# Attention feeding two MLPs on one core: the last double pair's sums first, six w_in blocks before the second batch, and a longer lead of w_in's products over w_out's

## The chip, the cores and the metric

The kernel runs on one core of a Trainium2 chip. The metric is the device time of one execution in microseconds, lower is better. TensorE multiplies into eight PSUM banks, VectorE, ScalarE and GpSimd do the elementwise work, and SyncE starts all DMA transfers. In the rows below they are PE (PEld is its weight load), DVE, ACT, POOL and SP.

## The reference

Two batches of 448 tokens, 12 heads of 64 columns; then two MLPs over all 896 tokens.

```python
scores = cap * tanh((q @ k.T) / sqrt(64) / cap)
attn   = exp(scores); attn = attn / (attn.sum(-1) + 1e-9)     # up to a common factor
x      = (attn @ v) heads side by side                         # 896 x 768
h      = x @ w_in                                              # 768 -> 2048
g      = (a0 + a1*h + a2*h**2 + a3*h**3) / (1 + |b0|*|h| + |b1|*h**2 + 1e-6)
x2     = g @ w_out                                             # 2048 -> 768
y      = max(x2 @ w1, x2 @ w2, x2 @ w3) @ w_out2               # 768 -> 768 -> 768
```

## The kernel before

**Number formats.** The MLP weights arrive as 64-bit floats. `weight()` loads a block of 128 x 768 into one of three `raw` buffers and decodes it on the chip: `scale` (L400 ScalarE or L402 GpSimd), `shift` (L406 VectorE), `rest` (L422 ScalarE or L425 VectorE), `sign` (L415 VectorE), a rounded high copy `wh...` (L441) and the remainder `wl...` (L430). Activations are split the same way, x into a high copy (L642) and a remainder (L646), g into `gh` (L745) and `gl` (L748). Each product of the MLPs is three matmuls: high by high, high by low, low by high.

**Attention** goes in six *double pairs* d of four heads each, d = 0 to 2 for batch 0 and 3 to 5 for batch 1. For each: six score tiles and one tile of the ends (L515, L522), tanh and exp on ScalarE (L536, L539, the tiles e_0 to e_6), the weighted values (L556, L575) into two banks that are copied to `xu` (L586), and the sums of the exponentials by a matmul with ones (L599, `summed`). The sums take a round trip: copied to a `row` buffer (L609), written to DRAM (`sums`), read back spread over the partitions (`comp`), inverted on VectorE (L617, L618), written to DRAM again (`rsum`), and read with a broadcast into two `row` buffers by four DMAs (`row<-rsum`). Then `scale` multiplies xu by the row (L638) and splits it into the two blocks of x of that double pair (L642, L646): d = 5 makes x_4 and x_5 of batch 1. All these DMAs, and the loads of `raw`, start in one order on SyncE.

**First MLP.** w_in is cut into 16 blocks fc of 128 columns; a *unit* is one block for one batch, 18 matmuls at L666 (`up`), two at a time over blocks of x. A unit's bank is read by ScalarE (L683, L686) and VectorE (L697, L700); L700, `second`, is the last reader, and only then another unit can use the bank. Two units together go through `rational` (L721 to L731) and `parts` (gh, gl). `down` multiplies them with w_out (L773): half "oa" runs between the units, half "ob" after all of them. The constant NG is the number of w_in blocks that batch 0 runs before batch 1 starts on the same blocks; LAG says how many pairs of units `up` runs ahead of `down`.

**The second MLP** (L861, L921) follows and isn't touched.

**Order.** The kernel doesn't write its engines' orders by hand. Each operation is added to `Flow` with an estimated cost on each engine that could do it; `Flow` derives due times, picks engine and buffer, and issues on each engine in the order it plans. TensorE's order follows the order of adding. `place` says which banks a value may use: once all scores are done, "h" (units) and "acc" may use any bank, "av" (weighted values and sums) only banks 4 and 5.

Of the kernel before, what the change touches and what calls it, by code (L numbers as in the profile page):

```python
# [17 lines left out]
B, H, S, D = 2, 12, 448, 64  # L18
# [9 lines left out]
GUARD = 1e-9  # L28
QGUARD = 1.0 + 1e-6
CAP = 6  # L30
NG = 4
LAG = 3
NSLOT, NRAW, NROW = 51, 3, 4
ND = NPAIR // 2
NFULL = S // P
# [35 lines left out]
class Flow:  # L71
# [11 lines left out]
    def add(self, engines, fn, after=(), vals=(), shared=False, due=None, leave=0, ahead=1e9, size=0.0, mode=None):  # L83
        first = next(iter(engines))
        if first == "pe":
            due = self.clock
            self.clock += engines["pe"]
        after = [a for a in after if a is not None]
        op = Op(engines, after, list(dict.fromkeys(vals)), fn, shared, due, leave, ahead, size, mode)
        for v in op.vals:  # L90
            v.users += 1
        for a in op.after:
            a.next.append(op)
        op.left = len(op.after)
        self.ops.append(op)
        return op

    def place(self, v, but=()):
        if v.kind not in ("sc", "av", "h", "acc"):
            free = self.free[v.kind]  # L100
            return (free[0],) if free else None
        done = self.scores == 0
        if v.kind == "sc":
            order = [(2 * i, 2 * i + 1) for i in ((0, 1, 3) if v.early else (0, 1))]
        elif done:
            order = [(4,), (5,)] if v.kind == "av" else [(i,) for i in range(8)]
        else:
            order = {"av": [(4,), (5,)], "h": [(6,), (7,)], "acc": []}[v.kind]
        order = [at for at in order if not any(self.banks[i] or i in but for i in at)]
        return min(order, key=lambda at: max(self.freed[i] for i in at)) if order else None  # L110
# [180 lines left out]
def attention_moe(ctx: ExitStack, tc: tile.TileContext, qk, v, w_in, w_out, w123, w_out2, par, out):  # L291
# [44 lines left out]
    def bank(val):  # L336
        return singles[val.at[0]]
# [4 lines left out]
    def dma(out_, in_, after=(), vals=(), size=0.0, issue=0.4, **kw):  # L342
        return add({"sp": issue}, lambda e: nc.sync.dma_start(out=out_(), in_=in_()), after, vals, size=size, **kw)  # L343
# [108 lines left out]

    units = [(fc, b) for b in range(B) for fc in range(NG)]
    units += [(fc, b) for fc in range(NG, NFC) for b in range(B)]
    NU = len(units)
    NK = NU // 2
    for n in range(NG):
        weight(("in", n), w_in[n])
        if n % 2:
            weight(("oa", n // 2), w_out[0, n // 2])  # L460
    for j in range(NG // 2, NFC // 2):
        weight(("in", 2 * j), w_in[2 * j])
# [14 lines left out]
    comp = [cp.tile([P, NG2], F32, name=f"comp{g}") for g in range(B * ND)]  # L477
# [70 lines left out]
    def weighted_rest(d):  # L548
        vr, got_v = VV[d]
        o = [Val("av", f"av{d}_{r}") for r in range(2)]  # L550
        x, ex = E[d, 2 * NFULL]

        def products(e):
            for r in range(2):
                for j in range(2):
                    pe.matmul(  # L556
                        bank(o[r])[j * D : j * D + D, :S], rest(vr, r, j), two(x)[r * D : r * D + D, j],
                        start=True, stop=False,
                    )

        done = add({"pe": FULL}, products, [ex, got_v], [*o, x, vr], mode="both")
        AV[d] = o, done
        XU[d] = slot(f"xu{d}"), []
        for c in last_copy[-2:]:
            c.before(done)

    def weighted(d, r):
        vr, got_v = VV[d]
        o, dep = AV[d][0][r], AV[d][1]
        es = [E[d, r * NFULL + n] for n in range(NFULL)]  # L570

        def products(e):
            for n, (x, _) in enumerate(es):
                for j in range(2):
                    pe.matmul(  # L575
                        bank(o)[j * D : j * D + D, :S], whole(vr, n, r, j), two(x)[:, j], start=False,
                        stop=n == NFULL - 1,
                    )

        dep = add(  # L580
            {"pe": NFULL * FULL}, products, [got_v, dep] + [ex for _, ex in es], [o, vr] + [x for x, _ in es],
            mode="halves",
        )
        xu, parts = XU[d]
        parts.append(add(
            {"dve": 0.54, "act": 0.43}, lambda e: copy_on[e](two(xu)[:, r], bank(o)[:, :S]), [dep], [o, xu]  # L586
        ))

    def summed(d):
        t, row = Val("av", f"sm{d}"), Val("row", f"sr{d}")  # L590
        es = [E[d, i] for i in range(2 * NFULL + 1)]

        def products(e):
            for n in range(NFULL + 1):
                for r in range(2):
                    x = es[r * NFULL + n if n < NFULL else 2 * NFULL][0]
                    for j in range(2):
                        g = (2 * r + j) * Q
                        pe.matmul(  # L599
                            bank(t)[g : g + Q, :S], ones[:, 0 if n < NFULL else 1 + r], two(x)[:, j], start=n == 0,  # L600
                            stop=n == NFULL, tile_position=(0, g),
                        )

        dep = add(
            {"pe": (NFULL + 1) * FULL}, products, [ex for _, ex in es] + [filled], [t] + [x for x, _ in es],
            mode="quarters",
        )
        got = add(
            {"act": 0.43, "dve": 0.54}, lambda e: copy_on[e](rows[row.at[0]], bank(t)[:, :S]), [dep], [t, row]  # L609
        )  # L610
        last_copy.append(got)
        flat_ = sums[d].rearrange("g s -> (g s)").rearrange("(p k) -> p k", p=P)
        out_ = dma(lambda: sums[d], lambda: rows[row.at[0]][0:P:Q], [got], [row], size=0.007, issue=0.4)
        back = dma(lambda: comp[d], lambda: flat_, [out_], size=0.007, issue=0.4)

        def recip(e):
            dve.tensor_scalar(out=comp[d], in0=comp[d], scalar1=guard, scalar2=None, op0=ALU.add)  # L617
            dve.reciprocal(out=comp[d], in_=comp[d])  # L618

        rc = add({"dve": 0.4}, recip, [back, guard_in])  # L620
        dst = rsum[d].rearrange("r j s -> (r j s)").rearrange("(p k) -> p k", p=P)
        wrote = dma(lambda: dst, lambda: comp[d], [rc], size=0.007, issue=0.4)
        for r in range(2):
            scale(d, r, wrote)

    def scale(d, r, wrote):
        xu, parts = XU[d]
        b, p = divmod(2 * d + r, NPAIR)
        row, x = Val("row", f"row{d}_{r}"), slot(f"x{b}_{p}", F32R)
        got = []  # L630
        for j in range(2):
            rr = slice(j * D, j * D + D)
            src = rsum[d][r, j : j + 1].broadcast_to([D, S])
            got.append(dma(lambda rr=rr: rows[row.at[0]][rr], lambda src=src: src, [wrote], [row], size=0.115, issue=0.4))
        u = lambda: two(xu)[:, r]
        m = add(
            {"dve": 0.54, "pool": 1.1},
            lambda e: engine[e].tensor_tensor(out=u(), in0=u(), in1=rows[row.at[0]], op=ALU.mult),  # L638
            [*got, *parts], [xu, row], shared=True,
        )  # L640
        hi = add(
            {"act": 0.47, "dve": 0.30}, lambda e: copy_on[e](two(x)[:, 0], u()), [m], [x, xu], shared=True,  # L642
        )

        def low(e):
            engine[e].tensor_tensor(out=two(x)[:, 1], in0=u(), in1=f32(two(x)[:, 0]), op=ALU.subtract)  # L646

        X[b, p] = x, add({"dve": 0.54, "pool": 1.1}, low, [hi], [x, xu], shared=True)
# [152 lines left out]
    for d in range(B * ND):  # L801
        for r in range(2):
            prep(2 * d + r)
        values(d)
        scores(d, 2 * NFULL)
        if d:
            weighted_rest(d - 1)
        for n in range(NFULL):
            scores(d, 2 * n)
            scores(d, 2 * n + 1)  # L810
            if d:
                weighted(d - 1, n) if n < 2 else summed(d - 1)
    table = add({"act": 1.3}, lambda e: act.preload_act_table_set("natural_log_exp_and_others"), last_tanh)
    early = 0
    weighted_rest(B * ND - 1)
    for j in range(2):
        up(early)
        early += 1
        weighted(B * ND - 1, j)
    summed(B * ND - 1)  # L820
    for n in range(early, 2 * LAG):
        up(n)
    for k in range(NK):
        parts(k)
        if k + LAG < NK:
            up(2 * (k + LAG))
            up(2 * (k + LAG) + 1)
        down("oa", 2 * k, 0)
# [163 lines left out]
```

## Time and profile before

| | |
|---|---|
| Time, median of three runs | 521.52 us (520.74 to 524.95) |
| The profiled execution's own time | 524.37 us |
| Its span, first to last instruction | 522.6 us |
| TensorE busy | 510.7 us (98%), 2637 matmuls |
| VectorE busy | 358.8 us (69%) |
| ScalarE busy | 295.1 us (56%) |
| GpSimd busy | 47.4 us (9%) |
| Mean granted clock of TensorE | 0.997 |

A time is that of the whole execution; the span leaves out 1.77 us before the first and after the last instruction. Shares are over the whole span: VectorE's 69% is an average of stretches where it is nearly always busy and of a last third where it is nearly idle.

### The profile page before, as it was taken

To read this page: it belongs to the slowest core of one execution; us is meant where nothing else is said; L and a number is where in the kernel's file an instruction comes from. 1 tells how busy PE (TensorE), PEld (TensorE's weight loads), DVE (VectorE), ACT (ScalarE), POOL (GpSimd) and SP (SyncE) were. 2 spreads that over 40 slices of the span, in tenths; PEclk is the share of its full clock that TensorE was granted. 3 is DMA by queue.
4 is the path that set the end of the run, shared out by engine and by line. 5 is a ranking of instruction groups with operands and counts; after the bars stand their busy time and mean duration, and the time that the engine had idled before them with its cause. 6 is when DMAs were issued, how large, how long until landed. Compare 5 with 4: busy or idle time off the path is not lost.

```text
span 522.6 us, 6706 instructions
## 1 busy us (share of the span) xinstructions
PE 510.7 (98%) x2637; PEld 418.0 (80%) x2637; DVE 358.8 (69%) x494; ACT 295.1 (56%) x407; POOL 47.4 (9%) x48
## 2 busy tenths in 40 slices
PE   8899999997999999999999999999999999999997
PEld 5333333676899889999997999999999999999996
DVE  0267999989999998788899999999842417111000
ACT  6999999956778866466766553474621121101111
POOL 0202303001201120101010200100000000000000
PEclk9999999999899999999999999999999999999999
DMA  8956755344101112000013678768400000000211
GB/s 308 365 181 217 243 180 212 111 156 154 62 0 61 60 61 60 1 1 2 1 61 99 217 251 279 249 210 271 176 0 2 0 1 0 1 0 10 80 64 61
DMA packets 16448, 58.37 MB, mean 112 GB/s; under 512 B 3592, under 2 KB 6944, under 8 KB 16416
## 3 DMA queue, kind: packets, MB, share of 16 engines
q1 hardware_dynamic: 16416, 57.94, 32.4%
q8 instruction: 20, 0.33, 0.3%
q14 instruction: 12, 0.10, 0.1%
HBM read 55.10 MB, written 2.84 MB: 111 GB/s over the span
## 4 chain that ended last, share of the span: by engine, by line
PE 60%; DVE 18%; DMA 9%; ACT 8%; issue 2%; SPq 2%; DVEq 0%; ACTq 0%
PE b L861 25%; PE b L773 16%; PE b L666 11%; PE b L921 8%; ACT e L536 4%; DMA rsum<-comp 3%; ACT e L539 3%; DMA row<-rsum 3%; SPq L343 2%; DVE W L697 2%; DMA comp<-sums 2%; DVE W L700 2%; DVE W L728 2%; DVE T L725 2%; DVE W L731 1%
## 5 line engine op out<-in xcount | busy, mean ns | idle before, releaser
L861 PE MATMUL b<-x,whm 128*128 128x448 f32 x432 | 122.6, 365 | 0.0
L666 PE MATMUL b<-x,whin 128*128 128x448 f32 x384 | 112.4, 373 | 2.7 <-DVE x L646 1.4
L861 PEld LDWEIGHTS b<-x,whm 128*128 128x128 f32 x432 | 81.1, 188 | 6.4
L666 PEld LDWEIGHTS b<-x,whin 128*128 128x128 f32 x384 | 72.4, 190 | 14.2 <-issue 3.0
L861 PE MATMUL b<-x,wlm 128*128 128x448 f32 x216 | 78.9, 365 | 0.0
L666 PE MATMUL b<-x,wlin 128*128 128x448 f32 x192 | 71.2, 371 | 0.0
L536 ACT ACTIVATE e<-b,qscale 128x448 f32<-128x448 f32 x84 | 49.0, 811 | 2.3 <-PE b L515 2.3
L889 ACT CAST h3h<-t 128x448 fp32r<-128x448 f32 x12 | 6.8, 567 | 66.8 <-DVE t L884 66.7
L539 ACT ACTIVATE e<-e,con 128x896 f32<-128x896 f32 x42 | 44.3, 1249 | 0.0
L861 PEld LDWEIGHTS b<-x,wlm 128*128 128x128 f32 x216 | 40.6, 188 | 3.2
L666 PEld LDWEIGHTS b<-x,wlin 128*128 128x128 f32 x192 | 36.5, 190 | 3.6
L773 PE MATMUL b<-gl,whoa 128*128 128x448 f32 x96 | 35.5, 369 | 2.2 <-DVE gl L748 2.2
L773 PE MATMUL b<-gh,wloa 128*128 128x448 f32 x96 | 35.2, 367 | 0.0
L773 PE MATMUL b<-gh,whoa 128*128 128x448 f32 x96 | 35.2, 367 | 0.0
L773 PE MATMUL b<-gh,whob 128*128 128x448 f32 x96 | 35.2, 366 | 0.0
L515 PE MATMUL b<-qk 64*128 64x448 f32 x144 | 33.6, 564 | 1.6 <-ACT e L536 1.4
L773 PE MATMUL b<-gh,wlob 128*128 128x448 f32 x96 | 35.1, 365 | 0.0
L773 PE MATMUL b<-gl,whob 128*128 128x448 f32 x96 | 35.1, 365 | 0.0
L686 ACT ACTIVATE W<-b,con 128x448 f32<-128x448 f32 x32 | 23.0, 719 | 18.6 <-PE b L666 18.5
L879 DVE TENSOR_TENSOR t<-b,t 128x448 f32<-128x448 f32 x12 | 7.5, 622 | 33.9 <-PE b L861 33.8
L515 PEld LDWEIGHTS b<-qk 64*128 64x128 f32 x144 | 14.3, 186 | 20.1 <-ACT e L536 9.5
L575 PE MATMUL b<-e,v 128*64 128x448 f32 x144 | 29.0, 545 | 0.0
(111 smaller groups left out, 917.7 us busy)
## 6 DMA issues: line engine op xcount, KB each, us to landing
raw<-in_w_out_dram SPq DMA_DIRECT2D x22, 768.0 KB, 4.4
raw<-in_w_dram SPq DMA_DIRECT2D x18, 768.0 KB, 4.2
raw<-in_w_in_dram SPq DMA_DIRECT2D x16, 768.0 KB, 6.0
qk<-in_qk_dram SPq DMA_DIRECT2D x12, 448.0 KB, 7.7
v<-in_v_dram SPq DMA_DIRECT2D x6, 448.0 KB, 11.9
row<-rsum SPq DMA_DIRECT2D x24, 112.0 KB, 3.6
out_dram<-ob SPq DMA_DIRECT2D x6, 384.0 KB, 2.8
out_dram<-ob SPq DMA_DIRECT2D x2, 192.0 KB, 1.9
```

The lines of the kernel that those rows point to most:

```text
L343: return add({"sp": issue}, lambda e: nc.sync.dma_start(out=out_(), in_=in_()), after, vals, size=size, **kw)
L515: pe.matmul(pair(t, j)[:, :S], k[rr], q[rr], start=True, stop=True)
L536: act.activation(two(x)[:, j], pair(t, j)[:, :S], AF.Tanh, scale=qscale)
L539: act.activation(two(x), two(x), AF.Exp, scale=cap)
L575: pe.matmul(bank(o)[j * D : j * D + D, :S], whole(vr, n, r, j), two(x)[:, j], start=False, stop=n == NFULL - 1,)
L666: pe.matmul(bank(h)[:, :S], w_, x_, start=cc == 0 and i == 0, stop=cc == NCC - 1 and i == len(terms) - 1)
L686: act.activation(two(w_)[:, i], bank(h)[:, :S], AF.Identity, bias=a2, scale=a3)
L697: dve.tensor_tensor(out=two(w_)[:, i], in0=bank(h)[:, :S], in1=two(w_)[:, i], op=ALU.mult)
L700: dve.scalar_tensor_tensor(out=two(w_)[:, i], in0=two(w_)[:, i], scalar=a1, in1=bank(h)[:, :S], op0=ALU.add, op1=ALU.mult)
L773: pe.matmul(bank(a)[:, :S], w_, g_, start=count[half, o, b] == 1, stop=count[half, o, b] == 3 * NFC)
L861: pe.matmul(bank(o)[:, :S], w_, x_, start=cc == 0 and i == 0, stop=cc == NCC - 1 and i == 2)
L921: pe.matmul(bank(o)[:, :NH], h_, w_, start=i == 0, stop=i == len(terms) - 1)
```

## The change

Four edits. NG goes from 4 to 6 and LAG from 3 to 4. After the scores, "av" values may use any bank. For the last double pair, one unit instead of two is run before the sums; the sums (`summed`) are added before the two weighted products instead of after them, and the scaling is split from `summed`, so that it is added after the weighted products. Elsewhere `summed` and `scale` stand one behind the other as before. The functions' lines from L619 on stand two lines lower in the changed kernel (L638 becomes L640, L666 becomes L668, L773 becomes L775).

```diff
-NG = 4
-LAG = 3
+NG = 6
+LAG = 4
@@ place
         elif done:
-            order = [(4,), (5,)] if v.kind == "av" else [(i,) for i in range(8)]
+            order = [(i,) for i in range(8)]
@@ summed(d)
-        wrote = dma(lambda: dst, lambda: comp[d], [rc], size=0.007, issue=0.4)
-        for r in range(2):
-            scale(d, r, wrote)
-
-    def scale(d, r, wrote):
+        return dma(lambda: dst, lambda: comp[d], [rc], size=0.007, issue=0.4)
+
+    def scale(d, wrote):
+        for r in range(2):
+            scale_pair(d, r, wrote)
+
+    def scale_pair(d, r, wrote):
@@ the double pairs
             if d:
-                weighted(d - 1, n) if n < 2 else summed(d - 1)
+                if n < 2:
+                    weighted(d - 1, n)
+                else:
+                    scale(d - 1, summed(d - 1))
 ...
     weighted_rest(B * ND - 1)
+    up(early)
+    early += 1
+    wrote = summed(B * ND - 1)
     for j in range(2):
-        up(early)
-        early += 1
         weighted(B * ND - 1, j)
-    summed(B * ND - 1)
+    scale(B * ND - 1, wrote)
     for n in range(early, 2 * LAG):
```

On TensorE, at the last double pair, the order before is this: weighted values into banks 85 and 86, six matmuls that end unit 1 (b_88, left out here) and six that begin unit 2, then the sums in bank 85.

```order
L575 MATMUL b_86<-e_3_754,v_499 64x448 x2
L575 MATMUL b_86<-e_4_770,v_499 64x448 x2
L575 MATMUL b_86<-e_5_795,v_499 64x448 x2
...
L666 MATMUL b_81<-x_1_480,whin_571 128x448 x2
L666 MATMUL b_81<-x_1_480,wlin_579 128x448
L599 MATMUL b_85<-e_0_682,ones 32x448 x2
L599 MATMUL b_85<-e_3_754,ones 32x448 x2
```

In the changed kernel at the same place:

```order
L668 MATMUL b_87<-x_5_662,wlin_416 128x448
L599 MATMUL b_81<-e_0_682,ones 32x448 x2
L599 MATMUL b_81<-e_3_740,ones 32x448 x2
...
L599 MATMUL b_81<-e_6_670,ones 32x448 x4
L575 MATMUL b_85<-e_0_682,v_495 64x448 x2
...
L575 MATMUL b_86<-e_5_785,v_495 64x448 x2
```

The sums stand right behind the last matmuls of unit 0, in bank 81, and the weighted values behind them.

On SyncE, from the write of the sums of d = 5 (sums_94) to the broadcast reads of its inverses (rsum_100), the order before is this; comp_106 is d = 5's, raw_... are loads of weights.

```order
L343 DMA sums_94<-row_80 4x448
L343 DMA raw_75<-in_w_in_dram 128x1536
L343 DMA comp_106<-sums_94 128x14
L343 DMA raw_74<-in_w_out_dram 128x1536
L343 DMA raw_76<-in_w_in_dram 128x1536
L343 DMA rsum_100<-comp_106 128x14
L343 DMA row_77<-rsum_100 64x448 x2
L343 DMA row_78<-rsum_100 64x448 x2
```

In the changed kernel from the read-back of d = 4 (comp_105) on:

```order
L343 DMA comp_105<-sums_93 128x14
L343 DMA raw_75<-in_w_in_dram 128x1536
L343 DMA sums_94<-row_78 4x448
L343 DMA rsum_99<-comp_105 128x14
L343 DMA raw_76<-in_w_out_dram 128x1536
L343 DMA comp_106<-sums_94 128x14
L343 DMA row_79<-rsum_99 64x448 x2
L343 DMA row_80<-rsum_99 64x448 x2
L343 DMA raw_74<-in_w_in_dram 128x1536
L343 DMA rsum_100<-comp_106 128x14
L343 DMA raw_75<-in_w_in_dram 128x1536
L343 DMA row_77<-rsum_100 64x448 x2
```

The round trips of d = 4 and d = 5 are now interleaved, with four loads of weights between the steps; a load waits for VectorE to have read that buffer's last block.

On VectorE, around the remainder of x_5 of batch 1 (the last step of d = 5), the order before is this.

```order
L638 TENSOR_TENSOR xu_863<-xu_863,row_77 128x448
L638 TENSOR_TENSOR xu_863<-xu_863,row_78 128x448
L725 SCALAR_TENSOR_TENSOR T_972<-T_972,qone,A_970 128x896
L646 TENSOR_TENSOR x_4_1065<-xu_863,x_4_1065 128x448
L646 TENSOR_TENSOR x_5_1068<-xu_863,x_5_1068 128x448
```

And in the changed kernel:

```order
L640 TENSOR_TENSOR xu_874<-xu_874,row_77 128x448
L727 SCALAR_TENSOR_TENSOR T_846<-T_846,qone,A_842 128x896
L699 TENSOR_TENSOR W_959<-b_83,W_959 128x448
L640 TENSOR_TENSOR xu_874<-xu_874,row_78 128x448
L702 SCALAR_TENSOR_TENSOR W_959<-W_959,con,b_83 128x448
L694 TENSOR_SCALAR T_980<-A_964,absb 128x448
L644 CAST x_5_1032<-xu_874 128x448
L730 SCALAR_TENSOR_TENSOR W_840<-W_840,con,A_842 128x896
L699 TENSOR_TENSOR W_1030<-b_84,W_1030 128x448
L648 TENSOR_TENSOR x_5_1032<-xu_874,x_5_1032 128x448
```

Six instructions of the MLP now stand between the second multiplication (L638, now L640) and the remainder of x_5, where one stood; and the multiplication itself has moved up: from the copy of the sums of d = 3 (the row `L609 ... row_78<-b_85`) to the remainder of x_5, VectorE's list has 71 instructions instead of 79.

## Rows read from the trace of the kernel before

**Rows 1.** What TensorE waits for, whole span: total us, times, longest.

```profile
PE b L773 <- DVE gl L748: 2.2, 2, 1.1
...
PE b L666 <- DVE W L700: 0.5, 2, 0.3
```

**Rows 2.** TensorE, 122 to 135 us: start, duration, line, and the idle time before.

```profile
122.29 0.37 PE L773 MATMUL b<-gh,whoa 128*128 128x448 f32 x1
123.75 0.47 PE L773 MATMUL b<-gl,whoa 128*128 128x448 f32 x1 [1.10 <-DVE gl L748]
...
125.52 0.37 PE L773 MATMUL b<-gh,whoa 128*128 128x448 f32 x1
...
127.79 0.37 PE L773 MATMUL b<-gh,wloa 128*128 128x448 f32 x1
128.97 0.47 PE L666 MATMUL b<-x,whin 128*128 128x448 f32 x1 [0.81 <-ACT x L642]
130.84 0.70 PE L666 MATMUL b<-x,whin 128*128 128x448 f32 x1 [1.40 <-DVE x L646]
...
131.71 0.95 PE L666 MATMUL b<-x,whin 128*128 128x448 f32 x2
...
134.54 0.37 PE L666 MATMUL b<-x,wlin 128*128 128x448 f32 x1
```

**Rows 3.** TensorE, the ends' weighted values of two double pairs.

```profile
74.67 1.69 PE L556 MATMUL b<-e,v 64*64 64x448 f32 x8
...
88.46 0.98 PE L556 MATMUL b<-e,v 64*64 64x448 f32 x8
```

**Rows 4.** Busy time of the engines in stretches.

```profile
core 0: us, PE busy (x) PEld busy (x) DVE busy (x) ACT busy (x) POOL busy (x), PEclk, DMA share, GB/s
74.00:131.00 57.00, 53.69 (x297) 33.20 (x297) 52.47 (x80) 44.47 (x58) 9.03 (x8) 1.00 0.50 170
131.00:185.00 54.00, 53.49 (x250) 47.89 (x251) 53.87 (x68) 42.12 (x58) 9.52 (x8) 0.97 0.13 44
...
120.00:140.00 20.00, 16.68 (x71) 14.19 (x70) 19.74 (x28) 12.32 (x20) 2.90 (x4) 0.91 0.30 107
```

**Rows 5.** TensorE at two late waits: unit 15's bank, and the last pair's gl.

```profile
184.56 0.68 PE L666 MATMUL b<-x,whin 128*128 128x448 f32 x2 [0.33 <-DVE W L700]
...
283.77 0.47 PE L773 MATMUL b<-gl,whoa 128*128 128x448 f32 x1 [1.15 <-DVE gl L748]
```

**Rows 6.** VectorE, 74 to 132 us, and unit 15's L700 at 183.83.

```profile
74.71 0.63 DVE L609 COPY row<-b 128x448 f32<-128x448 f32 x1
...
92.30 0.94 DVE L430 TENSOR_TENSOR wloa<-decoa,whoa 128x768 fp32r<-128x768 f32 x1
93.17 0.95 DVE L430 TENSOR_TENSOR wlin<-decin,whin 128x768 fp32r<-128x768 f32 x1
...
109.21 1.56 DVE L646 TENSOR_TENSOR x<-xu,x 128x448 fp32r<-128x448 f32 x1
...
130.17 1.15 DVE L646 TENSOR_TENSOR x<-xu,x 128x448 fp32r<-128x448 f32 x2
131.24 1.14 DVE L728 SCALAR_TENSOR_TENSOR W<-W,con,A 128x896 f32<-128x896 f32 x1
...
183.83 0.67 DVE L700 SCALAR_TENSOR_TENSOR W<-W,con,b 128x448 f32<-128x448 f32 x1
```

**Rows 7.** What VectorE waits for, 74 to 132 us.

```profile
DVE xu L638 <- DMA row<-rsum: 2.9, 5, 0.9
DVE decoa L406 <- POOL decoa L402: 0.7, 1, 0.7
DVE row L609 <- PE b L599: 0.3, 1, 0.3
DVE comp L617 <- DMA comp<-sums: 0.3, 1, 0.3
```

**Rows 8.** ScalarE ahead of the copy of the sums of d = 5.

```profile
111.53 0.93 ACT L400 ACTIVATE decin<-raw 128x768 f32<-128x768 f32 x1 [1.81 <-DMA raw<-in_w_in_dram]
112.34 0.53 ACT L609 COPY row<-b 128x448 f32<-128x448 f32 x1
```

**Rows 9.** Tile comp: reads of sums and writes of inverses, start to landing.

```profile
DMA to landing us min/median/max: 1.6/4.0/5.5
```

**Rows 10.** Tile row: writes of sums and broadcast reads of inverses.

```profile
DMA to landing us min/median/max: 2.7/3.6/5.2
```

## The prediction

> **What bounds the kernel now.** I read the waits first. TensorE is busy 98% of the span, so only its rests and slow stretches can be won. Behind 74 us, where the two orders part, TensorE waits for gl twice and for the bank of a unit twice [rows 1], and for x_4 of batch 1, at 128.97 for the high copy and at 130.84 for the remainder [rows 2]. Then the pitch of matmuls, from start to start: 11 steps from 125.52 to 127.79 are 0.206 us each. With it, the three gaps in rows 2 cost 123.75 − 122.29 − 0.21 = 1.25, 1.18 − 0.21 = 0.97 and 1.87 − 0.21 = 1.66 us. Behind the last one the matmuls are slow: 11 from 130.84 to 134.54 take 3.70 instead of 2.27 us, and the granted clock of 120 to 140 us is 0.91 [rows 4]. Of the two levels, 2.4 GHz and 1.2 GHz, that is the lower one for a few us, after the rests of TensorE from 122 on. It cost 1.43 us. One loss isn't shown as a wait: the ends' weighted values at 74.67 took 1.69 us, at 88.46 0.98, since their bank was still being copied: 0.7 us [rows 3]. Together 0.7 + 3.88 + 1.43 + 0.5 (banks) + 1.15 (the last gl, rows 5) = 7.7, with what lies between the rows some 8 us. **That is the most that this change can win, 1.5%.**
>
> Then the stretches [rows 4]: from 74 to 131 us VectorE is busy 52.5 of 57 us, and from 131 to 185 us 53.9 of 54. There it, and not TensorE, sets the pace: TensorE's units wait for VectorE's L700 to free a bank. A rest of TensorE that is taken away before 185 us comes back as a wait for VectorE at 185, unless VectorE's list itself gets there earlier. So the sum has to be made on VectorE.
>
> **VectorE's list up to x_5.** From the copy of sums at 74.71 to the remainder of x_5 of batch 1 the order has 79 instructions before and 71 after. By kinds, three of 896 elements fewer, six of 448 fewer, one shift fewer and two of 768 more. Prices from start to start [rows 6]: 768 elements 93.17 − 92.30 = 0.87; two of 448 131.24 − 130.17 = 1.07, so about 0.53; 896 about 1.05. The list gets shorter by 3 × 1.02 + 6 × 0.52 + 0.47 − 1.74 = 4.9 us. The whole list at such prices is 47.9 us before and 43.0 after. Before, it ended at 130.17 + 1.15 = 131.32, which is 8.7 us later than 74.71 + 47.9. Of these, 4.2 are waits [rows 7]; the other 4.5 are instructions that took longer than their kind (the L646 at 109.21 took 1.56, where a pair took 1.15, rows 6).
>
> **The waits of VectorE after.** The change puts the sums of d = 5 ahead of the weighted values, and ScalarE's copy no longer comes as late as 112.34, behind a load that it waited for [rows 8]. But SyncE's order now interleaves the round trips of d = 4 and d = 5 with four loads of weights, each of which waits until VectorE has read the last block of that raw buffer. What stands behind such a load waits too: the read-backs comp_105 and comp_106, the write rsum_99, rsum_100 and the broadcasts behind them. So I count what VectorE has to do between the instruction that frees the buffer and the one that needs the data, against the landing times.
> – comp_105: 4.5 us of work, against about 0.9 of issue and 1.6 to 5.5 of landing [rows 9]: a wait of 0 to 1.9 us.
> – comp_106: 4.4 us of work, the same: 0 to 2.0 us.
> – the broadcasts of d = 4, behind comp_106 on SyncE: 6 us of work, against 0.9 + 1.2 of issues and 2.7 to 5.2 of landing [rows 10]: 0 to 1.3 us.
> – d = 5: between the reciprocal and the first multiplication 7.7 us of work, against 0.4 + 4.0 (rsum, the median of rows 9) + 1.2 + 2.7 to 5.2: 0.6 to 3.1 us.
> Together 0.6 to 8.3 us. I take 5, above the middle, since the read-back that stood behind a load before is the one that took 5.5 us. The lengthening I leave at 4.5. VectorE then has x_5 at 74.7 + 43.0 + 9.5 = 127.2 us, 4 us earlier than before; with the bounds 122.8 to 130.5.
>
> **TensorE at x_5.** From 74 us to the first product with x_5 the attention matmuls are the same in both orders; of the MLP's there are 123 + 15 before and 129 after, 9 fewer, or 1.9 us. Before, that product started at 131.71 [rows 2]; without the losses ahead of it (0.7 + 3.88 + 0.46 of the slow clock) it would be at 126.7, and after at 124.8. Its remainder comes at 127.2. So TensorE rests some 2.3 us there, 0 to 5.7 with the bounds, and part of the clock's 1.4 us is lost again. The waits at 123.75 to 130.84 don't vanish: they become one wait for x_5, half as long.
>
> **Where VectorE sets the pace.** Before, TensorE reached the bank of unit 15 at 184.56 [rows 5], 7.6 us later than by its pitch alone from 74 us, and the L700 that it waited for came 11.7 us later than by the bare list (98.1 us from 74.71 to 184.5). So the lateness grew by 3.0 us from x_5 on. After, the last such place of this stretch is the bank of unit 17: VectorE's list up to there is 104.2 us, 6.1 longer, and TensorE has 36 matmuls more ahead of it, 7.4 us. That is 1.3 us of room won. VectorE's lateness after is 9.5 + 3.0 = 12.5. TensorE is then late by 7.6 + (12.5 − 11.7) − 1.3 = 7.1 us instead of 7.6. **Of the wins before 185 us 0.5 us are left**, whatever happens at x_5: an x_5 that comes in time only moves the wait. The bounds of VectorE's waits give 2.7 to 10.4, a win of 4.9 to a loss of 2.8.
>
> **The last gl.** Before, 67 matmuls lie between the last unit and the gl that is waited for at 283.77 (13.7 us at 0.204); with LAG 4 there are 73, 1.2 us more, against a wait of 1.15 [rows 5]. The chain from the last unit to its gl keeps its steps. I take the whole 1.15; if VectorE is fuller there, it is 0.
>
> **What costs nothing.** The table load, the free banks for "av" (the sums get bank 81 and no longer wait for a copy) and the 0.7 us of rows 3, which the order now covers by a score tile ahead of it, are all upstream of the bound at 185 us, so they give nothing of their own.
>
> **Sum.** 524.37 − 0.5 − 1.15 = 522.7 for an execution like the profiled one, which is 2.85 us over the median; so the median goes from 521.52 to **519.9 us**, 0.3% faster. About 1% is what a measurement of this kernel can tell from no change, so this is "the same".
>
> **Rivals.** (a) *The small transfers land early*, at 1.6 and 2.7 us instead of behind the loads' traffic. Then VectorE waits 0.6 us rather than 5, x_5 is there at 122.8, in time, TensorE is late by 2.7 at 185, and the end is won too: 4.9 + 1.15 = 6.0, 515.5 us, 1.2% faster. For it: the comp reads with no load just ahead took 1.6 us [rows 9]. Against it: the loads now stand just ahead in the order. The Trainium skill, in "DMA: Bandwidth & Descriptors", section "Anatomy of one DMA — SWDGE (gpsimd) path", gives one DMA a fixed cost of about 2.0 us plus its bytes over 436 GB/s, whatever else is queued. By it all four waits above would be nil, and the time, an estimate, about 515. The trace disagrees: the same 7 KB take from 1.6 to 5.5 us here; the measurement decides, and the rule's case has no more chance than this rival's 0.13.
> (b) *The exponential comes late.* ScalarE's order after has a decode (L400) just ahead of the last exp of d = 5, and the sums need that exp. If its load lands as late as the one in rows 8 (1.8 us of waiting, 0.8 of work), TensorE rests 2 to 3 us at the sums, and the chain of d = 5 and all of VectorE's later list slide by up to that, since it had been full. On top of the bounds' upper end: 2.8 + 2.5 and nothing from the last gl = 5.3 us slower, 526.8. It decides once that load holds ScalarE for 2.5 us. Chance of slower by over 1%: 0.05; of a loss below that: 0.2.
> (c) *Nothing moves*: VectorE's lateness grows by 2 to 3 us and eats both wins, 521.5. That lies in the main case's range.
>
> **Chances and range.** Main case with (c): 0.82, (a) 0.13, (b) 0.05. The range takes in most of the main case's bounds and leaves (a) and (b) out: 516.3 (a win of 5.2) to 523.2 (a loss of 1.7). Faster by over 1% 0.13, within 1% 0.82, slower 0.05.
>
> **What would show it.** In the trace after: no wait of 0.7 us at the ends' values; no wait for gl before 130 us; one wait for x of batch 1 at 124 to 128 us, of 1 to 5 us, with a lower clock behind it; VectorE over 97% busy from 125 to 185 us; waits for L700 at 170 to 187 us; no wait for the last gl. VectorE's waits for comp and row of d = 4 and 5 together near 5 us. I am wrong if TensorE doesn't rest between 120 and 187 us at all (then VectorE's list wasn't the bound), or if those waits are all near 0.

## Result and profile after: 527.1 us against 524.3, slower by 0.7%

The changed kernel takes 527.12 us (median of 13 runs, 525.13 to 530.05). The kernel before, run beside it, takes 524.26 us (13 runs, 520.74 to 525.47), more than the 521.52 of the three runs that the prediction started from. The ratio is 1.0072, with a 95% interval of 1.0047 to 1.0098. Here and below a ratio leaves out the slow runs, those over 1.5% above the fastest of the same kernel, and isn't the quotient of the medians: for p_after_110 the medians of all runs give 0.9960 in place of 0.9915, for p_before_110 0.9906 in place of 0.9883. The forecast was 519.9, 0.3% faster, with 523.2 as its upper end: wrong in sign and outside the range. The profiled execution of after takes 527.01 us, its span is 525.2, 2.6 longer than before.

What TensorE waits for in after, whole span (total, times, longest); it answers to [rows 1]:

```profile
PE b L668 <- DVE W L702: 6.7, 5, 4.2
PE b L515 <- ACT e L536: 1.4, 1, 1.4
PE b L380 <- DVE idle L348: 1.4, 1, 1.4
PE b L556 <- DVE row L609: 1.0, 1, 1.0
```

The waits for gl and for x of batch 1 are gone, as is the one behind the last unit. In their place there are five waits for L702 (L700 before), and one for L609 that the kernel before didn't have. Where they lie on TensorE (start, duration, idle before):

```profile
60.89 0.93 PE L556 MATMUL b<-e,v 64*64 64x448 f32 x4
62.82 0.97 PE L556 MATMUL b<-e,v 64*64 64x448 f32 x4 [1.01 <-DVE row L609]
...
126.73 0.99 PE L668 MATMUL b<-x,whin 128*128 128x448 f32 x2
...
174.38 0.37 PE L775 MATMUL b<-gh,wloa 128*128 128x448 f32 x1
178.91 1.12 PE L668 MATMUL b<-x,whin 128*128 128x448 f32 x2 [4.17 <-DVE W L702]
179.83 0.58 PE L668 MATMUL b<-x,wlin 128*128 128x448 f32 x1
...
184.68 0.66 PE L668 MATMUL b<-x,whin 128*128 128x448 f32 x2
...
193.45 0.68 PE L668 MATMUL b<-x,whin 128*128 128x448 f32 x2
...
215.23 0.67 PE L668 MATMUL b<-x,whin 128*128 128x448 f32 x2 [0.44 <-DVE W L702]
217.06 0.67 PE L668 MATMUL b<-x,whin 128*128 128x448 f32 x2 [0.34 <-DVE W L702]
229.18 0.67 PE L668 MATMUL b<-x,whin 128*128 128x448 f32 x2 [0.75 <-DVE W L702]
262.11 0.64 PE L668 MATMUL b<-x,whin 128*128 128x448 f32 x2 [1.03 <-DVE W L702]
```

The stretches of [rows 4], then the one behind them, whose row of before follows in a fence of its own (us, busy time of PE, PEld, DVE, ACT and POOL, granted clock, DMA share, GB/s):

```profile
74.00:131.00 57.00, 56.86 (x336) 36.06 (x329) 53.42 (x82) 45.60 (x67) 11.68 (x8) 1.00 0.55 168
131.00:185.00 54.00, 49.83 (x233) 45.69 (x232) 52.93 (x67) 39.58 (x55) 8.28 (x5) 0.94 0.06 16
185.00:250.00 65.00, 63.46 (x307) 56.85 (x306) 59.47 (x73) 39.10 (x54) 13.01 (x8) 1.00 0.18 61
```

```profile
185.00:250.00 65.00, 65.00 (x317) 59.03 (x316) 55.17 (x70) 41.26 (x57) 7.58 (x5) 1.00 0.08 25
```

From 74 to 131 us TensorE hardly rests now. Then comes a bill in one piece. From 174.38 to 178.91 it loses 4.53 − 0.20 = 4.3 us, and behind this rest 15 matmuls take 184.68 − 178.91 = 5.77 us where 15 × 0.203 = 3.0 would do: the clock is at its lower level (the granted clock of 131 to 185 us is 0.94, before 0.97), 2.7 us. Behind 185 us VectorE stays nearly full (59.5 of 65 us, 55.2 before), and TensorE waits for it another 2.6 us; with the slower steps just before and behind these rests it loses 4.0 there.

The long rest in the two engines that it came from, ScalarE first, then VectorE:

```profile
171.18 1.04 ACT L723 ACTIVATE A<-T,qone 128x896 f32<-128x896 f32 x1 [3.01 <-DVE T L707]
172.13 0.82 ACT L441 CAST whoa<-decoa 128x768 fp32r<-128x768 f32 x1
172.86 0.95 ACT L724 ACTIVATE A<-A 128x896 f32<-128x896 f32 x1
173.71 1.91 ACT L422 ACTIVATE raw<-raw 128x768 uint8<-128x768 uint8 x1
175.37 1.28 ACT L688 ACTIVATE W<-b,con 128x448 f32<-128x448 f32 x2
```

```profile
126.57 0.61 DVE L648 TENSOR_TENSOR x<-xu,x 128x448 fp32r<-128x448 f32 x1
...
177.12 1.15 DVE L699 TENSOR_TENSOR W<-b,W 128x448 f32<-128x448 f32 x2
178.19 1.26 DVE L702 SCALAR_TENSOR_TENSOR W<-W,con,b 128x448 f32<-128x448 f32 x2
...
192.72 0.67 DVE L702 SCALAR_TENSOR_TENSOR W<-W,con,b 128x448 f32<-128x448 f32 x1
```

TensorE had finished units 14 and 15 at 170.3. ScalarE's first step on them, L688, stands in its order behind L723, and that waited 3 us for a late L707 of VectorE; two steps of decoding (L441, L422) and L724 stand between them too. So L688 came at 175.37, L702 at 178.19, and the banks, the only two that units have left, at 178.8. VectorE's lateness had reached ScalarE's queue.

**The ledger of the two profiled executions**, at the same number of matmuls started. The changed kernel is 0.8 us behind at 60 us: the first twelve score matmuls take 3.66 us in after and 2.53 before; this differs between the profiles of all kernels here and is taken for chance. At 74 us it is 2.6 behind: 1.7 more, the rest for L609 and what lies around it. At 185 us it is 1.3 behind. So 1.2 were won from 74 to 185, and 1.1 of that is a shorter pitch of the matmuls (last section); the rests and the clock cost as much as before. At 262 us it is 4.2 behind: the 4.0 at the waits for L702, less 1.0 of pitch. At the start of the second MLP it is 2.9 behind (346.4 against 343.5 us), since the last gl is no longer waited for, and at the end 2.6.

### The profile page after: what moved, and what is told of

The parts are those of the page before. It is cut to its first block, busy times and chain, and to the rows that moved or that the text cites. A ratio compares the mean times of both kernels' runs of the same rounds, so it can differ in the third digit from the quotient of the medians.

```text
span 525.2 us, 6707 instructions
## 1 busy us (share of the span) xinstructions
PE 510.8 (97%) x2637; PEld 419.2 (80%) x2637; DVE 360.3 (69%) x495; ACT 292.9 (56%) x405; POOL 56.3 (11%) x49
## 4 chain that ended last, share of the span: by engine, by line
PE 57%; DVE 22%; ACT 10%; DMA 7%; issue 3%; SPq 0%; POOL 0%; DVEq 0%; POOLq 0%; ACTq 0%
PE b L867 25%; PE b L775 15%; PE b L927 8%; PE b L668 7%; ACT e L536 4%; ACT e L539 3%; DMA raw<-in_w_in_dram 3%; DMA comp<-sums 3%; DVE W L699 2%; DVE W L730 2%; DVE W L702 2%; DVE W L733 2%; DVE T L727 2%; DVE T L707 2%; DVE wlin L430 1%
## 5 line engine op out<-in xcount | busy, mean ns | idle before, releaser
L668 PE MATMUL b<-x,whin 128*128 128x448 f32 x384 | 112.5, 374 | 6.9 <-DVE W L702 6.7
L668 PEld LDWEIGHTS b<-x,whin 128*128 128x128 f32 x384 | 72.8, 192 | 17.8 <-DVE W L702 7.8
L668 PE MATMUL b<-x,wlin 128*128 128x448 f32 x192 | 71.3, 371 | 0.0
L536 ACT ACTIVATE e<-b,qscale 128x448 f32<-128x448 f32 x84 | 47.8, 751 | 4.6 <-PE b L515 4.5
L668 PEld LDWEIGHTS b<-x,wlin 128*128 128x128 f32 x192 | 36.8, 192 | 3.1
L775 PE MATMUL b<-gl,whoa 128*128 128x448 f32 x96 | 35.2, 367 | 0.1
L775 PE MATMUL b<-gh,whoa 128*128 128x448 f32 x96 | 35.1, 365 | 0.0
L775 PE MATMUL b<-gh,wloa 128*128 128x448 f32 x96 | 35.1, 365 | 0.0
L775 PE MATMUL b<-gh,whob 128*128 128x448 f32 x96 | 35.1, 365 | 0.0
L775 PE MATMUL b<-gl,whob 128*128 128x448 f32 x96 | 35.1, 365 | 0.0
L775 PE MATMUL b<-gh,wlob 128*128 128x448 f32 x96 | 35.1, 365 | 0.0
L723 ACT ACTIVATE A<-T,qone 128x896 f32<-128x896 f32 x16 | 16.7, 1044 | 24.8 <-DVE T L707 23.5
L688 ACT ACTIVATE W<-b,con 128x448 f32<-128x448 f32 x32 | 22.9, 717 | 11.9 <-PE b L668 11.9
```

Of the source, the lines that this page charges most:

```text
L536: act.activation(two(x)[:, j], pair(t, j)[:, :S], AF.Tanh, scale=qscale)
L668: pe.matmul(bank(h)[:, :S], w_, x_, start=cc == 0 and i == 0, stop=cc == NCC - 1 and i == len(terms) - 1)
L688: act.activation(two(w_)[:, i], bank(h)[:, :S], AF.Identity, bias=a2, scale=a3)
L723: ln = add({"act": 0.945}, lambda e: act.activation(two(a_), two(t_), AF.Ln, bias=qone), [da, db, table], [a_, t_])
L775: pe.matmul(bank(a)[:, :S], w_, g_, start=count[half, o, b] == 1, stop=count[half, o, b] == 3 * NFC)
```

## Experiments

Each was run beside the kernel before; ratios are to it, with 95% intervals. Runs of the kernel before range from 519.6 to 530.2 us, so single profiles show where, and ratios how much.

**Undoing one edit at a time**, in the changed kernel: NG back (e1_ng4), LAG back (e2_lag3), the last pair's order back (e3_oldlast); and two units instead of one ahead of the sums (c1).

```diff
@@ e1_ng4
-NG = 6
+NG = 4
@@ e2_lag3
-LAG = 4
+LAG = 3
@@ e3_oldlast
-    up(early)
-    early += 1
-    wrote = summed(B * ND - 1)
     for j in range(2):
+        up(early)
+        early += 1
         weighted(B * ND - 1, j)
-    scale(B * ND - 1, wrote)
+    scale(B * ND - 1, summed(B * ND - 1))
@@ c1
-    up(early)
-    early += 1
+    for _ in range(2):
+        up(early)
+        early += 1
     wrote = summed(B * ND - 1)
```

> The changed kernel with NG back at 4, all else as changed. Theory A (the loss is made of two things: VectorE decodes weights ahead of the copy of the sums of d = 2 near 60 us, which the new order of the last double pair brings by moving due times, about 1.7 us; and TensorE's waits for L702 at 179 and 215 to 262 us, 6.7 us with 2.8 of lower clock behind them, which the lead and the six blocks bring): VectorE's list here has the same decode ahead of that copy, so a wait of about 1 us at 60 to 63 us stays; unit 14's L702 stands at 91.7 us of VectorE's bare list instead of 92.1, so the wait near 179 stays at 3 to 5 us: 525 to 528. Rival B (the six blocks alone make the loss): back to the time before, 523 to 524.5.

523.21 us, ratio 1.0008 (0.9971 to 1.0045).

> The changed kernel with LAG back at 3. Theory A: the wait of about 1 us at 60 to 63 us stays (same list on VectorE up to there). The L702 of unit 14 is at 95.7 us of VectorE's bare list, 3.6 us later than with LAG 4, but TensorE has 36 matmuls of w_out ahead of it that were behind: 7.4 us of room; so the waits for L702 shrink to under 2 us, and waits for gl (2 us) come back: 523 to 526. Rival C (the longer lead is what costs): 521 to 524. Rival B (the six blocks): 526 to 528, as changed.

526.36 us, 1.0056 (1.0021 to 1.0092), with 2.2 us of waits for L702 and 2.9 for gh and gl in its profile.

> The changed kernel with the last double pair in its old order (unit, weighted, unit, weighted, sums). Theory A: VectorE's list up to the copy of the sums of d = 2 is that of the kernel before, so no wait at 60 to 63 us and TensorE stands about 1.7 us earlier at the first score tile of d = 5 than in the changed kernel (74 to 75 us); x_5 comes later (its remainder is at 45.7 us of the bare list instead of 43.0), a rest of 0 to 3 us near 125; total 523 to 527. Rival D (the early 1.7 us are a matter of chance from run to run, such as the first loads): the wait at 60 to 63 us is there all the same, in this kernel or in the kernel before.

527.05 us, 1.0072 (1.0034 to 1.0110).

> The changed kernel with two units instead of one ahead of the sums of the last double pair, the sums still ahead of the weighted values. Theory A: no wait at 60 to 63 us (VectorE's list up to there is that of the kernel before), x_5 still early (40.0 us of the bare list), unit 14's L702 at 89.8 us instead of 92.1, so the wait near 179 falls from 4.2 to about 2 us: 2 to 4 us faster than the changed kernel, 523 to 525, level with or just below the kernel before. Rival D: same time as the changed kernel, 526 to 528.

528.20 us, 1.0081 (1.0052 to 1.0111).

By the times, the whole loss goes with the six blocks: rival B. Theory A fell in two points. The rest for L609 near 62 us isn't the last pair's doing: e3_oldlast and c1 have the kinds of instruction of the kernel before on VectorE just ahead of that copy, and rest there 1.3 and 1.0 us all the same, while e1_ng4 doesn't, with the changed pair. And an L702 2.3 us earlier in the list, in c1, left the long rest at 4.7 us.

**One edit alone, in the kernel before**, and the cause by shortening VectorE's work. In e5_after_short and e6_before_short `newton` computes 8 of 896 columns and leaves out the rest, so g is not the reference's; the orders stay as they are.

```diff
@@ b1_ng6
-NG = 4
+NG = 6
@@ b2_lag4
-LAG = 3
+LAG = 4
@@ e5_after_short, e6_before_short
-            dve.scalar_tensor_tensor(out=two(t_), in0=two(t_), scalar=qone, in1=two(a_), op0=ALU.add, op1=ALU.mult)
+            tt, aa = two(t_)[:, 0, :8], two(a_)[:, 0, :8]
+            dve.scalar_tensor_tensor(out=tt, in0=tt, scalar=qone, in1=aa, op0=ALU.add, op1=ALU.mult)
```

> The kernel before with NG = 6 and nothing else. Theory B2 (the six blocks alone make the loss: TensorE runs five or six units ahead in banks that the first products of w_out for batch 1 take away later, and then rests in one piece until VectorE has caught up, so that its clock falls too): a rest of 3 to 5 us for L700 between 165 and 185 us with a lower clock behind it, 526 to 528. Rival E (the six blocks cost only together with the new order of the last double pair): 523 to 525.

528.52 us in four runs, 1.0108 (1.0037 to 1.0178).

> The kernel before with LAG = 4 and nothing else. Theory B2: the lead is no part of the loss; the wait for the last gl (1.15 us before) is gone, the rest as before: 522 to 524.5. Rival C (the lead costs): 525 to 527.

524.93 us, 1.0023 (0.9989 to 1.0057): no loss that can be told. But its profile isn't "the rest as before". The wait for the last gl is gone, and the waits for L700 are 5.2 us instead of 0.5, one of them 2.9 at 168 us with a lower clock behind it (0.94 from 131 to 185 us):

```profile
PE b L666 <- DVE W L700: 5.2, 5, 2.9
```

In e2_lag3, six blocks without the longer lead, none for L702 is over 0.8. So a long rest near 170 to 180 us comes with the lead alone too, and its size in one profile doesn't tell the time.

> The changed kernel with one of VectorE's instructions cut short: `newton` (L727) works on 8 of its 896 columns, so g isn't the reference's; all orders stay word for word. VectorE's list is 0.9 us shorter for each pair of units, seven of them before 179 us, 6 us. If VectorE's lateness is what the rest at 179 and the later waits for L702 come from, the rest of 4.2 falls below 1 us, no lower clock follows it, and the sum of the L702 waits falls from 6.7 to below 1.5: 518 to 521. If they come from a chain that doesn't hang on VectorE's work (the banks' order or ScalarE's), the rest at 179 stays at 3 us or more: 525 to 527.

519.94 us, 0.9909 (0.9867 to 0.9951).

> The kernel before with the same instruction cut short in the same way (g isn't the reference's). The waits for x_4 of batch 1 near 129 us hang on the round trip of the sums and stay, 1 to 2 us of rests and some clock; the waits for L700 and the last gl go: 519 to 522. With VectorE out of the way the changed kernel should be level with this one or 1 to 3 us faster, instead of 3.7 slower.

519.23 us, 0.9918 (0.9886 to 0.9951).

What TensorE waits for in e5_after_short, without the first 20 us' rows:

```profile
PE b L556 <- DVE row L609: 1.1, 1, 1.1
...
PE b L668 <- DVE W L702: 0.6, 2, 0.3
```

Same order, shorter VectorE: 6.7 us of waits for L702 become 0.6, the rest at 179 is gone, the granted clock of the profile is 1.000, and changed and unchanged kernel are level. So the rests, and the loss in time, hang on VectorE's lateness, and not on the order of the banks by itself. In b1_ng6 the six blocks alone bring a rest for L700 at 187 us (2.64), beside 3.3 us of rests for x. These the last pair's new order removes where six blocks follow (e3_oldlast without it: 4.9, after: none); with four blocks e1_ng4 still has 2.1.

**More and fewer blocks**, in the kernel before.

```diff
@@ n2
-NG = 4
+NG = 2
@@ n8
-NG = 4
+NG = 8
```

> The kernel before with NG = 2. If the loss grows with the number of blocks that batch 0 runs before batch 1 (six: 527 to 529, four: 523.5), two blocks are level with four or faster, 520 to 524; x of batch 1 is wanted some 7 us earlier than with four blocks, though, so the rests for x_4 near 125 grow to 4 us or more, and if these set the time it is slower, 525 to 528. The two readings are told apart by the rests for x and for L700 in its trace.

527.19 us, 1.0087 (1.0055 to 1.0120).

> The kernel before with NG = 8. If the loss grows with the number of blocks, 528 to 531, with no rest for x of batch 1 and one rest for L700 of over 3 us. If six blocks were an unlucky place of the planner's, 523 to 526.

528.58 us, 1.0120 (1.0086 to 1.0154).

Two blocks are as bad as six, and not by the rests for x: these are 1.4 us in sum, those for L700 2.8 and for gl 1.8. So no straight line leads from the number of blocks to the time, and four is where the order happens to fit the chip. The time of n2 lies in the range that its expectation gave for late x, but its trace doesn't bear that reason out; n8 has five rests for L700 (7.1 us), not one.

**The planner's prices.** The rests come from VectorE being late. If the planner's prices for it are too low, its orders count on VectorE too early, so here the planner counts more for it; no instruction computes anything else.

```diff
-                    dur = op.engines[e]
+                    dur = op.engines[e] * (1.10 if e == "dve" else 1.0)
```

> The changed kernel, where the planner counts 1.10 times the estimated cost for every instruction on VectorE while it makes the orders; no instruction changes what it computes. In the traces VectorE's instructions take about that much longer than planned (a 768-wide one 0.95 for 0.87, some 1.6 beside GpSimd). If TensorE's rests for L702 come from VectorE being later than the plan, the orders now put copies and casts on the other engines and keep ScalarE's part of a unit ahead of what waits for VectorE: sum of L702 waits below 4 us, no long rest, 522 to 525. If they come from the six blocks' use of the banks alone, still 526 to 528.

520.43 us, 0.9915 (0.9871 to 0.9960). The time is below the expected range, but the sign in the trace failed: one long rest for L702 is there, 4.1 us at 177:

```profile
PE b L668 <- DVE W L702: 4.1, 1, 4.1
```

> The kernel before with the same 1.10 on VectorE's planned costs. If VectorE's lateness against the plan sets TensorE's rests there too, 520 to 523; if the round trip of the sums for x_4 does, no change: 523 to 524.5.

517.63 us, 0.9883 (0.9838 to 0.9928), the lowest median here, and faster than both kernels.

What TensorE waits for in p_before_110 (all of it), and its two stretches:

```profile
PE b L515 <- ACT e L536: 1.4, 1, 1.4
PE b L380 <- DVE idle L348: 1.4, 1, 1.4
```

```profile
131.00:185.00 54.00, 54.00 (x268) 50.05 (x268) 50.76 (x66) 43.49 (x62) 9.36 (x6) 1.00 0.08 27
185.00:250.00 65.00, 65.00 (x322) 60.26 (x321) 57.83 (x74) 48.88 (x62) 14.55 (x9) 1.00 0.17 52
```

Behind 20 us the view lists no rest of TensorE. VectorE's busy time falls from 358.8 to 350.3 us, ScalarE's rises from 295.1 to 305.0 and GpSimd's from 47.4 to 60.3: six `rest` steps of the decoding and some copies have changed engines. ScalarE waits much less for VectorE's L705 (L707 in after). From 74 to 284 us, in before, after and p_before_110:

```profile
ACT A L721 <- DVE T L705: 14.9, 10, 3.3
ACT A L723 <- DVE T L707: 23.5, 11, 3.6
ACT A L721 <- DVE T L705: 4.9, 3, 2.5
```

What the new order gives and what VectorE's 8.5 us less of work give isn't told apart by a run of its own; e6_before_short, with 14.6 us less of VectorE's work in the old order, gains no more (0.9918).

**The same prices with the edits apart**: four blocks and all else as before with 1.20 (p_before_120), the six blocks alone (q_ng6_110), the changed kernel with four blocks (p_e1_110), and that with LAG 3 too (q_lastpair_110).

```diff
@@ q_ng6_110, from p_before_110
-NG = 4
+NG = 6
@@ p_e1_110, from p_after_110
-NG = 6
+NG = 4
@@ q_lastpair_110, from p_e1_110
-LAG = 4
+LAG = 3
@@ p_before_120, from p_before_110
-                    dur = op.engines[e] * (1.10 if e == "dve" else 1.0)
+                    dur = op.engines[e] * (1.20 if e == "dve" else 1.0)
```

> The kernel before with NG = 6 and VectorE's planned costs times 1.10. If six blocks have a cost of their own (batch 1's sums take the banks in one place and TensorE has to let VectorE catch up there): a rest of 2 us or more for L700 between 170 and 190 us, and 2 to 4 us above the same kernel with four blocks (517.6): 520 to 522. If the loss was only a bad fit to the prices: 516.5 to 519 and no long rest.

518.49 us, 0.9888 (0.9810 to 0.9965).

> The changed kernel with NG = 4 and VectorE's planned costs times 1.10: the longer lead and the new last double pair, without the six blocks. If these two were worth something that VectorE's lateness hid, 513 to 516.5; if they are neutral, as LAG = 4 alone was, 516.5 to 519.

519.74 us, 0.9919 (0.9874 to 0.9964).

> The changed kernel with NG = 4 and LAG = 3, so with the new last double pair and any bank for its sums alone, and VectorE's planned costs times 1.10. No rest for x of batch 1; if that is worth something 513 to 516.5, else 516.5 to 519.

517.79 us, 0.9896 (0.9822 to 0.9970).

> The kernel before with VectorE's planned costs times 1.20. If 1.10 is already past what the chip takes, ScalarE and GpSimd become the late ones and it is slower than with 1.10: 518 to 522; if not, 515 to 517.5.

520.37 us, 0.9956 (0.9915 to 0.9997).

All of TensorE's waits behind 20 us in q_ng6_110:

```profile
...
PE b L666 <- DVE x L646: 0.4, 1, 0.4
PE b L773 <- DVE wlob L430: 0.3, 1, 0.3
PE b L773 <- ACT whob L441: 0.2, 1, 0.2
```

With 1.10 six blocks have no cost of their own that shows: the rest for L700 is gone, and 518.5 can't be told from 517.6. Nor do the lead and the new last pair bring anything that can be told (517.8 to 519.7). In q_lastpair_110 the rests for x that were to go are 1.9 us, and p_e1_110's 519.74 lies above both of its ranges. 1.20 is too much: gl and gh come late now (3.4 us of waits).

## Why the prediction was wrong

**Right, by its own steps.** VectorE, not TensorE, set the pace, and a rest taken away early came back at a unit's bank. VectorE's lateness at the bank of unit 17 was put at 12.5 and is 12.4: L702 there ends at 193.39, and 76.8 + 104.2 is 181.0. TensorE's was put at 7.1 and is 4.3 + 2.7 + 0.4 = 7.4, and the win up to there at 0.5; with the pitch left out it is 0.1. In part this is luck, two errors that cancel: at x_5 VectorE is 7.4 late instead of 9.5 (list 43.0 from 76.8 to 127.2), and from there on it loses 5.0 instead of 3.0. The instructions' lengthening up to x_5 was put at 4.5, and 7.4 less 3.0 of waits is 4.4. The wait for the last gl went and gave about what was counted (1.15; the changed kernel gains 1.3 there). That the remainder of x_5, forecast for 127.2, ended at 126.57 + 0.61 = 127.18 is luck too: its list began 2.1 us later, and the waits were 2.0 smaller.

**Wrong in these terms**, the step that failed first.
– *The end of the sum: "the last such place of this stretch is the bank of unit 17", and behind 185 us only the last gl.* **This is the step that failed**: what VectorE costs behind 185 us was put at nothing. The sum needed no place there, because in the trace of before VectorE had caught up by then; I had looked up only how full it was from 74 to 185. In after its lateness doesn't end there: four more waits for L702 from 215 to 262 us, 2.6 us by the view and 4.0 with the steps around them, against 0.5 that was to be won before. Ahead of it the rest had another place too: it came at the bank of unit 14, 4.3 us in one piece and 2.7 of the lower clock, and at that of unit 17 TensorE went on at 193.45 almost without one.
– *The start of the sum: only "behind 74 us, where the two orders part".* TensorE's orders part there, VectorE's at its 24th row: the six blocks change which weights are decoded first, and so does the longer lead alone (b2_lag4). The 1.7 us at 60 to 64 us lie there, a term put at nothing. Under the planner's own prices the rest for L609 is in all kernels with six blocks and the changed line of `place` (1.0 to 1.3 us); it is 0.4 in b1_ng6 and n8, 0.2 in n2, and missing in the three with four blocks. That it belongs to the blocks' number is a pattern, not tried by itself.
– *VectorE's waits of 5 us* for the round trips were mis-sized: 1.6 of them, 3.0 with the other waits. This term erred to the good side. The transfers of the tile comp land like this in after (compare [rows 9]):

```profile
DMA to landing us min/median/max: 1.4/3.7/4.7
```

  The landing was hardly shorter, so most of it must be the work that stood between. The Trainium skill's figure ("DMA: Bandwidth & Descriptors", section "Anatomy of one DMA — SWDGE (gpsimd) path"), about 2.0 us for so small a transfer, is given there for transfers that GpSimd starts. Those here are started by SyncE, and the trace of after shows the same as that of before: some land faster, half of them in 3.7 us or more.
– *"TensorE rests some 2.3 us" at x_5* (its own terms give 127.2 − 124.8 = 2.4): it came 2.6 us later than counted, for what had happened ahead of 74 us, and hardly rested (the pair at 126.73 takes 0.99 for 0.57).
– *Priced list plus slip* treats an order as a queue on one engine. The trace shows more: ScalarE's L688 for units that were done stood behind L723, which waited for VectorE, and behind decoding. Between units' end and banks' release lay 8.5 us. A sum over VectorE's list has no term for it.

The rivals named a late exponential and small transfers; neither happened: the exponential held TensorE not at all, and rival (a), with transfers in time, nearly did come true, without its win, since VectorE lost that time again behind x_5. None of them was what happened. That the loss hangs on VectorE's lateness is shown by shortening its work in the same order. That the planner's prices for VectorE are too low, so that its orders fit the chip with four blocks and badly with two, six and eight, is the best reading: the six kernels planned with 1.10 or 1.20 have ratios of 0.988 to 0.996, the nine others that compute everything 1.001 to 1.012. It isn't shown alone, since a higher price also takes work off VectorE. Why four fits better than two stays open; so does the rest of 4.1 us in the profile of p_after_110, which is of its slowest execution (526.0 us), slow for another reason: its matmuls have the longer pitch (last section).

A smaller fault was the start of the sum: the median of before is 521.52 in three runs, and 522.5 to 524.3 in the sets of 13 to 31 runs beside which the other kernels were timed.

## What to carry to other kernels

When a planner writes the orders, check its prices against the trace first: counting 10% more for one engine that is nearly full gained about 1% here, with four blocks as with six, and beside it none of the edits of the order gained anything that can be told. An order that follows estimates can fail through the in-order queues: a late engine holds up a second one that has something ready and urgent standing behind. And a sum on the engine that sets the pace must begin where that engine's order changes and go on to the end of its work. Up to 185 us this one came out; the loss lay before and behind. What the lower clock costs can't be read off a rest's length: 2.7 us behind 4.2 in after, 1.6 behind 4.1 in p_after_110, 1.4 behind three short ones before.

## What was not expected of the hardware

The same matmul has two pitches at the full granted clock. In after, 36 of them go from 141.14 to 148.43 us, 0.2025 each; before, 11 from 125.52 to 127.79, 0.206 [rows 2]. Before has the longer pitch, 0.2067, from about 108 to 172 us and from 185 to 262, after only from about 194 to 216.

```profile
141.14 0.56 PE L668 MATMUL b<-x,whin 128*128 128x448 f32 x2
...
148.43 0.36 PE L775 MATMUL b<-gh,whoa 128*128 128x448 f32 x1
```

Over some 500 matmuls that is 2 us, as much as many a wait, and no view names it. The profile of p_after_110 has the longer pitch from 181 us to the end of the second MLP, some 1400 matmuls or 5.6 us; that of p_before_110 has the shorter one from 128 us on. From 290 to 440 us TensorE is always busy in both, at a granted clock of 1.00, with 728 matmuls in the one and 742 in the other:

```profile
290.00:440.00 150.00, 150.00 (x728) 136.24 (x727) 107.30 (x145) 62.12 (x73) 5.87 (x4) 1.00 0.41 137
290.00:440.00 150.00, 150.00 (x742) 139.07 (x741) 104.18 (x143) 58.12 (x69) 5.72 (x5) 1.00 0.38 129
```

So two profiles can differ by 6 us without any wait. The ten runs of p_before_110 lie in two groups about 6 us apart, 513.5 to 515.2 and 520.1 to 521.5; that this is the pitch isn't shown, since only one of them has a profile. The cause of the two pitches is open. Also, profiles of kernels that start alike show the first twelve score matmuls in 2.53 to 4.85 us, after a wait for the first loads of up to 0.9.
